# Stacking the left-over rows of two more groups in the Fourier stage of a spectral + gated block

## The chip, the cores and the metric

The kernel runs on one core of one Trainium2 chip. The metric is the device time of one execution in microseconds (us), given as the median of several executions. The core has five engines that run their own instruction lists and meet at semaphores: TensorE (PE in the profile, with its weight loads as PEld), VectorE (DVE), ScalarE (ACT), GpSimd (POOL) and SyncE (SP), which here only starts DMA transfers. The engines' work areas are SBUF (128 partitions of ordinary on-chip memory) and PSUM (where TensorE writes its sums).

## The reference

`x` is 2048 x 640 in float32. The block normalises each row, takes a two-dimensional real Fourier transform over rows and features, multiplies by a complex filter, transforms back and adds the result to `x`. A gated layer with a residual follows.

```python
def _A_ref(x, w_r, w_i):
    B, S, D = x.shape
    X = jnp.fft.rfft2(x, axes=(-2, -1))
    X = X * (w_r + 1j * w_i)
    return jnp.fft.irfft2(X, s=(S, D), axes=(-2, -1))

h = x + _A_ref(_layernorm(x), A_w_r, A_w_i)                     # D = 640, 321 frequencies
n = _layernorm(h)
h2 = h + ((n @ B_w_gate) * (n @ B_w_up)) @ B_w_down             # 640 -> 1728 -> 640
```

## The kernel before

All transforms are matrix products with constant tables. The program has four stages: a first transform along the rows for 16 tiles of 128 rows (`s1_mm`, L263), the feature stage that the change touches, the transform back along the features and rows, and the gated layer, which takes the larger part of the time. The order of every engine's instructions is the order in which the Python code calls the helpers; nothing reorders them afterwards. A semaphore wait stands in front of an instruction where its data or its buffer needs one, and an engine that waits holds up everything behind that instruction in its list. SP's list is such a list too: a transfer that must wait holds back the later ones.

**Left-over rows.** After the first transform the features are cut into four classes (even or odd, real or imaginary part) of about 160 rows. 128 rows of each fill a matrix operand (`s1`), and some 32 rows of each are left over. `s1_rest` (L292) puts the left-overs of all four classes together into the 128 partitions of `rest`. So that a faster format of matrix product keeps float32's accuracy there, ACT rounds them to a high part (`rest_high`, L299) and DVE forms the low part by a subtraction (`rest_low`, L302). Both lie in `s1r`: 128 partitions x (high or low) x 16 groups x 128 columns.

**The feature stage.** It runs over 16 groups of 128 columns. For group g:
- `d_mm(g)` (L428) is the transform along the features: four products from `s1` (the profile shows them as `im<-tab,s` and `re<-tab,s`), then the left-over rows. A group that has no entry in `ST` takes six products of 322 columns from `s1r` (high and low part against a table in two parts; `re<-frt,s1r`). A group with an entry in `ST` takes four products of 160 to 194 columns from a *stacked* operand (`re<-frt,st`), in which each class has the high part, the low part and the high part again under one another in 99 partitions.
- `d_out(g)` (L460) copies the result to SBUF on ACT (tile `t`).
- `s2_mm(g)` (L467) is the rest of the transform along the rows; for groups 1 to 13 it writes the PSUM tile `u`, of which there is one (`bufs=1`, L473).
- `filt(g)` (L478) multiplies by the filter on DVE, in three instructions that read `u` and the filter tile `wts` (L484 to L486); the closure it returns adds the two products, `y + us` (L493): on GpSimd for group 0, on DVE for the others.
- `is2_mm(g)` (L514) starts the way back; `is2_parts(g)` (L547) copies its sums out: `high` and `end` on ACT (L545), `low` on DVE (L563), `main` on ACT (L556), `edges` on GpSimd.

A round g of the loop at L583 calls `s2_mm(g)`, `d_mm(g+2)`, `is2_mm(g-1)`, then `filt(g)`, and behind it the copies and the sum. In round 0 ACT makes the high part for groups 10 to 15, in round 1 DVE makes their low part. The tile `qr`, into which `high` and `low` write, lies in the same memory as `rest`, so `high(0)` must wait until DVE has read `rest` for the last time.

**How the stacked operand is made.** A stacked operand needs rows in other partitions than they were computed in, and the kernel moves them through device memory: `spread(a, b)` (L443) writes the left-over rows of groups a to b-1 to the buffer `sfar` with four transfers of 66 pieces, `stack(g, n, ...)` (L448) reads n groups back with two transfers, of 264 and 132 pieces. A piece is as long as the number of groups in the call times 512 bytes. All are started by SP, between the loads of the matrices `mm` (`bits` in the profile) and of the filter (`load_w`, L407).

```python
PLAIN, MID = 5, 10
AGAIN = {0: (5, 3, "dC"), 1: (8, 2, "qt"), 4: (10, 3, 0), 7: (13, 3, 1)}
```

Groups 0 to 4 are not stacked. Groups 5 to 9 are written ahead of the loop, groups 10 to 15 in round 2. `AGAIN` says in which round which groups are read back, and to which memory.

Of the kernel before, what the change touches and what calls it, by code (L numbers as in the profile page):

```python
# [12 lines left out]
F32R = mybir.dt.float32r  # L13
AF = mybir.ActivationFunctionType
OP = mybir.AluOpType

P = 128
S, D, NF, FF = 2048, 640, 321, 1728
NT = S // P
NG = 16  # L20
# [6 lines left out]
RW = (160, 194, 162, 162)  # L27
PLAIN, MID = 5, 10
IPLAIN, IFAR = 5, 9
SUMS = 7  # L30
IPARTS = ((5, 4), (9, 3), (12, 4))
AGAIN = {0: (5, 3, "dC"), 1: (8, 2, "qt"), 4: (10, 3, 0), 7: (13, 3, 1)}
NR = 4
# [16 lines left out]
def f32(ap):  # L50
    return ap.bitcast(F32)
# [29 lines left out]
def tile_spectral_glu(ctx: ExitStack, tc: tile.TileContext, x, wre, wim, wgu, wlast, wdown, wdlast,  # L81
                      cc, ci, fmain, frem, imain, irem, mm, out):
    nc = tc.nc
# [52 lines left out]
    def home(tag, shape, name, dt=F32):  # L136
        return keep.tile(shape, dt, tag=tag, name=name)
# [11 lines left out]
    s1r = home("wA", [P, 2, NG, P], "s1r", F32R)  # L149
# [250 lines left out]
    s1_rest(NT - 1)  # L400
    for a, b in ((0, 2), (2, PLAIN), (PLAIN, MID)):
        rest_high(a, b)
        rest_low(a, b)
# [39 lines left out]
    def spread(a, b):  # L443
        for q, (r, s) in enumerate(RROWS):
            nc.sync.dma_start(sfar[q, :, :, a - PLAIN:b - PLAIN].rearrange("l r g n -> r l g n"),
                              f32(s1r[r:r + 32 * s + 1:s, :, a:b]))

    def stack(g, n, tag):  # L448
        if tag in (0, 1):
            o = s1r[:, tag, NG - 12:NG].rearrange("p (q n) m -> p q n m", q=4)  # L450
        else:
            o = home(tag, [P, 4, n, P], "st", F32R)
        src = sfar[:, :, :, g - PLAIN:g - PLAIN + n].rearrange("q l r g n -> q (l r) (g n)")
        for a, b, r in ((0, 66, 0), (66, 99, 0)):
            nc.sync.dma_start(f32(o[a:b].rearrange("p q g n -> p q (g n)")),
                              src[:, r:r + b - a].rearrange("q r n -> r q n"))
        for i in range(n):
            ST[g + i] = o[:, :, i]
# [19 lines left out]
    def filt(g):  # L478
# [11 lines left out]
        else:  # L490
            for h in range(2):
                products(h, PU[g][h][:, 0:NQ])
        return lambda: (tt if g else nc.gpsimd.tensor_tensor)(y, y, us, op=OP.add)  # L493

# [78 lines left out]
    for g in range(4):  # L573
        for way in range(2):
            load_mm(g, way)
        if g < 3:
            load_w(g)
    spread(PLAIN, MID)
    d_mm(0)
# [3 lines left out]
    for g in range(NG - 1):  # L583
# [32 lines left out]
        if g + 3 < NG:  # L616
            load_w(g + 3)
        if g >= 4 and g in AGAIN:
            stack(*AGAIN[g])
        if g == 0:  # L620
# [4 lines left out]
        if g + 2 < NG:  # L625
# [7 lines left out]
            if 1 <= g < NG - 3:  # L633
                low()
                main(slice(0, 4))
                edges(nc.gpsimd)
        if g < 2:
            stack(*AGAIN[g])
        elif g == 2:
            spread(MID, NG)  # L640
        if g == 9:
# [920 lines left out]
```

## Time and profile before

| | |
|---|---|
| median of 3 executions | 671.65 us (671.63 to 671.98) |
| the profiled execution, its own time | 671.61 us |
| its span, first to last instruction | 669.8 us |
| TensorE busy in the span | 660.0 us (99%) |
| TensorE in the chain that ended last | 95% of the span |
| granted TensorE clock | 1.00 throughout |
| feature stage | from about 38 us to 106 us |
| round with six left-over products (rounds 1 and 2) | 4.45 us each |
| round with four (rounds 3 and 4) | 3.99 and 3.98 us |

The time of the profiled execution is 1.8 us more than its span; that part lies outside the instructions that the profile shows. A row of the timeline view gives the start in the span, the duration, the engine, the source line, the operation, its tiles (output, arrow, inputs), shape and count; in brackets the engine's idle time before it and what ended it. A row of the windows view gives for one stretch of time the busy time of each engine with its number of instructions, then the granted clock, the mean share of the 16 DMA engines that was busy, and GB/s. "SPq" rows are transfers being started, not transferred.

### The profile page before, as it was taken

The numbers are of one execution on the slowest core, as the hardware profiler recorded it, in microseconds if no ns is written. First come the engines' busy times: TensorE is split into PE (matmuls) and PEld (weight loads), VectorE is DVE, ScalarE is ACT, GpSimd is POOL, SyncE is SP. The second block draws the span as 40 slices with busy tenths as digits, with TensorE's granted clock in tenths as the row PEclk, the third lists the DMA queues.
The fourth block names the chain that finished last, engine by engine and source line by source line (L and its number), as shares of the span: only waits on it lengthen the run. The fifth ranks groups of instructions, "written<-read, shape, count | busy, mean of one in ns | idle before, by whom it ended". The sixth has DMA issues, their size and how long they took to land.

```text
span 669.8 us, 10242 instructions
## 1 busy us (share of the span) xinstructions
PE 660.0 (99%) x3695; PEld 587.1 (88%) x3695; DVE 468.7 (70%) x951; ACT 321.6 (48%) x621; POOL 394.5 (59%) x379
## 2 busy tenths in 40 slices
PE   6999999999999999999999999999999999999997
PEld 6999999887888888888888899888888888888887
DVE  6969997788767767594857567754757475757644
ACT  6977773585525243453626146634434251624220
POOL 3101124750397977969686445198786869697610
PEclk9999999999999999999999999999999999999999
DMA  8639885502212120042332467212011121212004
GB/s 320 226 109 282 237 252 160 160 1 79 79 40 80 39 79 28 34 99 59 99 78 84 93 134 260 78 41 74 13 37 76 41 78 40 79 40 80 1 0 158
DMA packets 48953, 66.12 MB, mean 99 GB/s; under 512 B 24082, under 2 KB 30670, under 8 KB 48774
## 3 DMA queue, kind: packets, MB, share of 16 engines
q1 hardware_dynamic: 48246, 62.91, 30.5%
q0 software_dynamic: 288, 2.16, 0.8%
q8 instruction: 29, 0.48, 0.3%
q10 hardware_dynamic: 368, 0.39, 0.2%
q14 instruction: 22, 0.18, 0.1%
HBM read 54.61 MB, written 10.84 MB: 98 GB/s over the span
## 4 chain that ended last, share of the span: by engine, by line
PE 95%; ACT 2%; DVE 1%; DMA 1%; issue 0%; POOL 0%; DVEq 0%
PE e L121 50%; PE d L121 26%; PE eo L121 4%; PE y L121 2%; PE re L121 2%; PE u L476 2%; PE im L527 2%; PE im L121 2%; PE im L270 2%; PE ir L527 1%; DMA x<-in_x_dram 1%; ACT s L296 1%; ACT fold L212 0%; ACT fold L211 0%; PE y L803 0%; PE u L527 0%
## 5 line engine op out<-in xcount | busy, mean ns | idle before, releaser
L121 PE MATMUL e<-xt,wst 128*128 128x512 f32 x864 | 211.1, 390 | 0.0
L121 PEld LDWEIGHTS e<-xt,wst 128*128 128x128 f32 x864 | 160.6, 188 | 31.7
L1082 DVE TENSOR_TENSOR x<-d,x 128x320 f32<-128x320 f32 x280 | 120.5, 483 | 41.2 <-PE d L121 37.0
L121 PE MATMUL d<-wd,ht 128*128 128x320 f32 x832 | 142.2, 309 | 0.0
L121 PEld LDWEIGHTS d<-wd,ht 128*128 128x128 f32 x832 | 129.6, 188 | 5.2
L996 POOL TENSOR_TENSOR wst<-raw,wst 128x1024 fp32r<-128x1024 f32 x23 | 55.5, 2412 | 69.5 <-ACT wst L995 69.5
L121 PE MATMUL e<-t,wst 128*128 128x512 f32 x360 | 94.0, 391 | 0.0
L121 PEld LDWEIGHTS e<-t,wst 128*128 128x128 f32 x360 | 66.7, 188 | 13.0
L121 PE MATMUL d<-wt,ht 128*128 128x320 f32 x360 | 69.0, 309 | 0.0
L1012 POOL TENSOR_TENSOR wst<-raw,wst 128x896 fp32r<-128x896 f32 (+1 forms) x46 | 65.3, 1444 | 0.2 <-ACT wst L1007 0.2
L121 PEld LDWEIGHTS d<-wt,ht 128*128 128x128 f32 x360 | 57.3, 188 | 0.8
L1098 ACT ACTIVATE ht<-e 128x512 fp32r<-128x512 f32 x44 | 26.4, 599 | 49.2 <-DVE e L1160 23.7
L1007 ACT ACTIVATE wst<-raw 128x896 fp32r<-128x896 f32 (+1 forms) x48 | 30.1, 676 | 31.2 <-POOL raw L1001 30.5
L1156 DVE TENSOR_TENSOR e<-e,h 128x512 f32<-128x512 f32 x24 | 16.8, 699 | 39.3 <-ACT wst L1007 23.1
L1057 DVE TENSOR_TENSOR x<-d,x 128x320 f32<-128x320 f32 x62 | 27.5, 485 | 22.4 <-PE d L121 22.3
L688 ACT ACTIVATE wd<-draw 128x320 fp32r<-128x320 f32 (+1 forms) x30 | 15.7, 560 | 55.1 <-POOL draw L698 52.4
L121 PE MATMUL e<-xt,wdir 128*128 128x512 f32 x180 | 42.1, 392 | 0.0
L1136 ACT ACTIVATE h<-e 128x512 f32<-128x512 f32 x24 | 14.3, 596 | 56.8 <-PE e L121 56.8
L121 PEld LDWEIGHTS e<-xt,wdir 128*128 128x128 f32 x180 | 33.4, 188 | 7.7 <-ACT xt L813 0.5
L1101 DVE TENSOR_TENSOR ht<-e,ht 128x512 fp32r<-128x512 f32 x54 | 37.0, 686 | 1.6 <-ACT ht L1098 1.3
L1153 ACT ACTIVATE h<-e 128x512 f32<-128x512 f32 x24 | 14.3, 598 | 46.7 <-PE e L121 46.7
L667 POOL TENSOR_TENSOR wd<-draw,wd 128x640 fp32r<-128x640 f32 x8 | 12.4, 1576 | 40.8 <-ACT wd L666 40.8
(239 smaller groups left out, 1188.1 us busy)
## 6 DMA issues: line engine op xcount, KB each, us to landing
raw<-in_wgu_dram SPq DMA_DIRECT2D x24, 640.0 KB
draw<-in_wdown_dram SPq DMA_DIRECT2D x24, 320.0 KB
wts<-in_wre_dram SPq DMA_DIRECT2D x16, 322.0 KB
x<-in_x_dram SPq DMA_DIRECT2D x15, 320.5 KB
out_dram<-x SPq DMA_DIRECT2D x15, 320.0 KB
bits<-in_mm_dram SPq DMA_DIRECT2D x32, 128.0 KB
wts<-in_wim_dram SPq DMA_DIRECT2D x9, 322.0 KB
zfar<-zr SPq DMA_DIRECT2D x32, 80.0 KB
```

Of the source, the lines that this page charges most:

```text
L121: nc.tensor.matmul(o, l, r, start=start, stop=stop, skip_group_check=True)
L527: nc.tensor.matmul(out, y[:, h, a:b], inv(g, h), start=n == 0, stop=n == len(ys) - 1)
L688: act(o[:, 0, a:a + n], src, AF.Copy)
L996: ptt(wa[:, 1], stage[:, 0:1024], f32(wa[:, 0]), op=OP.subtract)
L1007: act(ws[:, 0, o:o + b - a], stage[:, a:b], AF.Copy)
L1012: ptt(ws[:, 1, o:o + b - a], stage[:, a:b], f32(ws[:, 0, o:o + b - a]), op=OP.subtract)
L1057: tt(xv, ps[b][:, 0:320], xv, op=OP.add)
L1082: tt(xv, o, xv, op=OP.add)
L1098: act(hop[:, a, 0], src, AF.Copy)
L1101: engine.tensor_tensor(hop[:, a, 1], src, f32(hop[:, a, 0]), op=OP.subtract)
L1136: act(h0, oa, AF.Copy)
L1156: tt(ob, ob, h1, op=OP.add)
```

## The change

Groups 3 and 4 become stacked groups as well.

- `PLAIN` is 3 instead of 5. The rows of groups 3 to 5 are written first, by four transfers, then read back at once in two calls (group 3 alone, then groups 4 and 5), and only then are the rows of groups 6 to 9 written. All of it stands on SP ahead of the loop. For this, high and low parts are made in the order (0, 1), (3, 4, 5), (2), (6 to 9).
- The other calls are cut anew: groups 6 and 7 are read in round 1, 8 in round 2, 9 to 11 in round 3, 12 to 14 in round 6, 15 in round 9. The rows of groups 10 to 15 are still written in round 2, from an earlier place in the code of that round, which is the same place in SP's list: behind the filter load of the round.
- A stacked operand can now be written in parts (`SH` keeps the tile, `at` gives the place). The transfers' shapes are those of before, but for the number of groups in them.
- The sum of group 1 is on GpSimd instead of DVE.

```diff
-PLAIN, MID = 5, 10
+PLAIN, NEXT, MID = 3, 6, 10
-AGAIN = {0: (5, 3, "dC"), 1: (8, 2, "qt"), 4: (10, 3, 0), 7: (13, 3, 1)}
+FIRST = ((3, 1, "dC", 0), (4, 2, "dC", 1))
+AGAIN = {1: ((6, 2, "qt", 0),), 2: ((8, 1, "dC", 0),), 3: ((9, 3, 0, 0),), 6: ((12, 3, 1, 0),), 9: ((15, 1, "dC", 0),)}
...
-    for a, b in ((0, 2), (2, PLAIN), (PLAIN, MID)):
+    for a, b in ((0, 2), (PLAIN, NEXT), (2, PLAIN), (NEXT, MID)):
         rest_high(a, b)
         rest_low(a, b)
...
-    def stack(g, n, tag):
-        if tag in (0, 1):
-            o = s1r[:, tag, NG - 12:NG].rearrange("p (q n) m -> p q n m", q=4)
-        else:
-            o = home(tag, [P, 4, n, P], "st", F32R)
-        src = sfar[:, :, :, g - PLAIN:g - PLAIN + n].rearrange("q l r g n -> q (l r) (g n)")
-        for a, b, r in ((0, 66, 0), (66, 99, 0)):
-            nc.sync.dma_start(f32(o[a:b].rearrange("p q g n -> p q (g n)")),
-                              src[:, r:r + b - a].rearrange("q r n -> r q n"))
+    SH = {}
+
+    def stack(g, n, tag, at):
+        if tag not in SH:
+            SH[tag] = s1r[:, tag, NG - 12:NG].rearrange("p (q n) m -> p q n m", q=4) if tag in (0, 1) else home(
+                tag, [P, 4, 3 if tag == "dC" else n, P], "st", F32R)
+        o = SH[tag][:, :, at:at + n]
+        src = sfar[:, :, :, g - PLAIN:g - PLAIN + n].rearrange("q l r g n -> (l r) q (g n)")
+        for a, b in ((0, 66), (66, 99)):
+            nc.sync.dma_start(f32(o[a:b].rearrange("p q g n -> p q (g n)")), src[0:b - a])
...
-        return lambda: (tt if g else nc.gpsimd.tensor_tensor)(y, y, us, op=OP.add)
+        return lambda: (tt if g > 1 else nc.gpsimd.tensor_tensor)(y, y, us, op=OP.add)
...
-    spread(PLAIN, MID)
+    spread(PLAIN, NEXT)
+    for job in FIRST:
+        stack(*job)
+    spread(NEXT, MID)
     d_mm(0)
...
-        if g >= 4 and g in AGAIN:
-            stack(*AGAIN[g])
+        if g == 2:
+            spread(MID, NG)
+        if g >= 4:
+            for job in AGAIN.get(g, ()):
+                stack(*job)
...
-        if g < 2:
-            stack(*AGAIN[g])
-        elif g == 2:
-            spread(MID, NG)
+        if g < 4:
+            for job in AGAIN.get(g, ()):
+                stack(*job)
```

The order of instructions on SP, from the end of the first loads into round 1, before (`sfar<-s1r` writes the left-over rows, `st<-sfar` reads them back; `bits` are the matrices, `wts` the filter):

```order
L445 DMA sfar<-s1r 33x2x640 x4
L417 DMA bits<-in_mm_dram 128x256
L410 DMA wts<-in_wre_dram 128x644
L455 DMA st<-sfar 66x4x384
L455 DMA st<-sfar 33x4x384
L417 DMA bits<-in_mm_dram 128x256 x2
L410 DMA wts<-in_wre_dram 128x644
```

and with the change:

```order
L446 DMA sfar<-s1r 33x2x384 x4
L458 DMA st<-sfar 66x4x128
L458 DMA st<-sfar 33x4x128
L458 DMA st<-sfar 66x4x256
L458 DMA st<-sfar 33x4x256
L446 DMA sfar<-s1r 33x2x512 x4
L418 DMA bits<-in_mm_dram 128x256
L411 DMA wts<-in_wre_dram 128x644
L418 DMA bits<-in_mm_dram 128x256 x2
L411 DMA wts<-in_wre_dram 128x644
```

Four reads and four writes now stand ahead of the matrix of group 4 and the filter of group 3 (the first `bits` and `wts` rows), where one set of four writes stood.

DVE in rounds 1 and 2, before, from the first filter product of group 1 to that of group 2:

```order
L484 TENSOR_TENSOR y<-u,wts 128x644
L485 SCALAR_TENSOR_TENSOR us<-u,wts 64x644
L486 TENSOR_TENSOR us<-u,wts 64x644
L303 TENSOR_TENSOR s1r<-rest,s1r 128x768
L493 TENSOR_TENSOR y<-y,us 128x644
L563 TENSOR_TENSOR qr<-ir_647,qr 64x32x8
L484 TENSOR_TENSOR y<-u,wts 128x644
```

and with the change:

```order
L486 TENSOR_TENSOR y<-u,wts 128x644
L487 SCALAR_TENSOR_TENSOR us<-u,wts 64x644
L488 TENSOR_TENSOR us<-u,wts 64x644
L304 TENSOR_TENSOR s1r<-rest,s1r 128x768
L565 TENSOR_TENSOR qr<-ir_653,qr 64x32x8
L486 TENSOR_TENSOR y<-u,wts 128x644
```

The sum `y<-y,us` of group 1 is gone from here; GpSimd's list has it behind the sum of group 0.

TensorE in round 1, `d_mm(3)` and what follows it, with the change (before, the four rows with `st` were six rows with `s1r`, 128x322 each):

```order
L478 MATMUL u<-t,bits 128x322 x2
L122 MATMUL im<-tab,s_89 128x160
L122 MATMUL re<-tab,s_89 128x193
L122 MATMUL im<-tab,s_89 128x161
L122 MATMUL re<-tab,s_89 128x161
L122 MATMUL im<-frt,st 128x160
L122 MATMUL re<-frt,st 128x194
L122 MATMUL im<-frt,st 128x162
L122 MATMUL re<-frt,st 128x162
L529 MATMUL ir_653<-bits,y 65x32x4 x2
```

Here `u` is `s2_mm(1)`, `ir` the beginning of `is2_mm(0)`.

## The prediction

> **What bounds the kernel now.** I read first the windows of rounds 1 to 4, then what TensorE waits for, then each engine's timeline in rounds 1 to 3.
>
> ```profile
> 45.58:50.03 4.45, 4.45 (x33) 4.12 (x31) 3.75 (x6) 2.60 (x6) 1.55 (x1) 1.00 0.66 174
> 50.03:54.48 4.45, 4.45 (x32) 4.12 (x31) 4.29 (x7) 3.36 (x8) 0.74 (x2) 1.00 0.95 288
> 54.48:58.47 3.99, 3.99 (x31) 3.66 (x29) 3.56 (x6) 2.79 (x7) 0.74 (x2) 1.00 0.93 246
> ...
> PE eo L121 <- POOL qr L560: 0.3, 1, 0.3
> ```
>
> TensorE is busy for the whole of each round, and the last row is the only wait of TensorE between 30 and 200 us: the stage runs at TensorE's speed, at a clock of 1.00. But round 2 has DVE busy for 4.29 of 4.45 us, so it is nearly a second bound, and the DMA engines are at 0.95.
>
> ```profile
> 47.70 0.42 PE L121 MATMUL re<-frt,s1r 128*128 128x322 f32 x1
> ...
> 52.16 0.42 PE L121 MATMUL re<-frt,s1r 128*128 128x322 f32 x1
> ...
> 53.16 0.60 PE L527 MATMUL ir<-bits,y 128*65 128x128 f32 x4
> 53.59 1.06 PE L527 MATMUL im<-bits,y 128*128 128x128 f32 x8
> ...
> 54.48 1.25 PE L476 MATMUL u<-t,bits 128*128 128x322 f32 x4
> ...
> 56.61 0.35 PE L121 MATMUL im<-frt,st 99*128 99x160 f32 x1
> ...
> 57.13 0.60 PE L527 MATMUL ir<-bits,y 128*65 128x128 f32 x4
> ```
>
> Matmuls overlap, so a block's cost is the distance from its first start to the next block's. Group 4's six left-over products take 53.16 - 52.16 = 1.00 us; group 5's four stacked ones 57.13 - 56.61 = 0.52 us.
>
> **The change part by part.**
>
> *Fewer products on TensorE.* 1.00 - 0.52 = 0.48 us for each of groups 3 and 4, on the path: 0.96 us at most. (The rounds say nearly the same: 4.45 - 3.99 = 0.46.) Whether all of it is kept depends on the tile `u`, of which there is one.
>
> ```profile
> 48.57 0.82 DVE L486 TENSOR_TENSOR us<-u,wts 64x644 f32<-64x644 f32 x1
> 49.42 0.96 DVE L303 TENSOR_TENSOR s1r<-rest,s1r 128x768 fp32r<-128x768 f32 x1
> 50.29 0.82 DVE L493 TENSOR_TENSOR y<-y,us 128x644 f32<-128x644 f32 x1
> 51.16 0.42 DVE L563 TENSOR_TENSOR qr<-ir,qr 64x256 fp32r<-64x256 f32 x1
> 51.61 0.83 DVE L484 TENSOR_TENSOR y<-u,wts 128x644 f32<-128x644 f32 x1
> ...
> 53.32 0.82 DVE L486 TENSOR_TENSOR us<-u,wts 64x644 f32<-64x644 f32 x1
> ...
> 55.77 0.83 DVE L484 TENSOR_TENSOR y<-u,wts 128x644 f32<-128x644 f32 x1 [0.32 <-PE u L476]
> ...
> 50.47 0.38 ACT L545 ACTIVATE qr<-ir 64x256 fp32r<-64x256 f32 x1 [0.84 <-DVE s1r L303]
> ...
> 52.06 0.60 ACT L556 ACTIVATE qm<-im 128x512 f32<-128x512 f32 x1
> ```
>
> DVE runs without a gap here and lets go of `u` at 53.32 + 0.82 = 54.14. TensorE writes `u` for group 3 at 54.48, only 0.34 later. With both savings it would come at 54.48 - 0.96 = 53.52 and find `u` still in use.
>
> *The sum moved to GpSimd* takes 50.29 to 51.11 out of DVE's list, but DVE does not gain 0.82 us. Its next instruction, L563 of group 0, needs `high(0)` on ACT, and that waits (the bracket) for DVE's L303, which ends at 49.42 + 0.96 = 50.38 as before: `high(0)` stays at 50.47 to 50.85. Handing over cost 0.09 us there (50.38 to 50.47), so L563 starts at about 50.93 instead of 51.16: 0.23 us earlier. `filt(2)` behind it keeps its length, so `u` comes free at 54.14 - 0.23 = 53.91, and TensorE, with a hand-over of 0.05 to 0.1, writes it at about 54.0. Before that was 54.48, so **0.48 us of the 0.96 are kept**, and TensorE stands for some 0.45 us ahead of `s2_mm(3)`. That is the new wait I expect.
>
> Is the rest of it lost later, or won back? `filt(3)` then waits for TensorE's `u` as it does at 55.77, and the whole pattern runs 0.48 us earlier: `u` is free again 2.53 us behind that start (51.61 to 54.14 in round 2), and TensorE is back 3.99 us after its last `u`. Nothing is late twice, nothing is regained. One smaller wait disappears inside the first: `is2_mm(1)` would write its `im` bank at 53.59 - 0.96 = 52.63, and ACT's `main(0)` reads the bank of group 0 until 52.66.
>
> *GpSimd's new sum* is priced by the old one, and by a pair of rows from a later stage:
>
> ```profile
> 46.33 1.55 POOL L493 TENSOR_TENSOR y<-y,us 128x644 f32<-128x644 f32 x1 [18.11 <-DVE us L486]
> ...
> 110.30 0.50 DVE L755 TENSOR_TENSOR yt<-q 128x322 f32<-128x322 f32 x1
> ...
> 110.35 1.06 POOL L763 TENSOR_TENSOR yt<-q 128x318 f32<-128x318 f32 x1 [1.62 <-DVE q L759]
> ...
> 128.77 0.75 POOL L763 TENSOR_TENSOR yt<-q 128x318 f32<-128x318 f32 x1
> ```
>
> It starts when DVE's L486 ends (48.57 + 0.82 = 49.39) and takes 1.55 us: 50.95. Beside it runs DVE's L303. Where GpSimd's L763 starts 0.05 us behind a DVE sum of two SBUF operands, it takes 1.06 us, else 0.75, so I let it lose the overlap with L303 too, up to 0.92 us: 51.9. `is2_mm(1)` needs the sum at 53.16 - 0.96 = 52.20. It stays hidden, and the waits around `u` would cover another 0.45 us; if that cover were gone, each further 0.1 us would cost 0.1.
>
> *Group 3's rows in time?* This is the unknown that matters: they are due at 47.70, in round 1.
>
> ```profile
> 40.39 0.83 DVE L303 TENSOR_TENSOR s1r<-rest,s1r 128x640 fp32r<-128x640 f32 x1
> ...
> 41.25 2.54 SPq L445 DMA_DIRECT2D sfar<-s1r  x4
> ...
> 45.26 0.35 SPq L410 DMA_DIRECT2D wts<-in_wre_dram  x1
> 46.63 0.75 SPq L455 DMA_DIRECT2D st<-sfar  x2
> ...
> 106.52 1.91 SPq L716 DMA_DIRECT2D ifar<-qr  x4
> 108.48 0.57 SPq L719 DMA_DIRECT2D ifar<-qr  x1
> 110.54 0.30 SPq L727 DMA_DIRECT2D xt<-ifar  x1
> ...
> 121.06 0.32 SPq L727 DMA_DIRECT2D si<-ifar  x1
> ...
> 121.00:122.00 1.00, 1.00 (x9) 1.00 (x9) 0.96 (x3) 0.27 (x1) 1.00 (x2) 1.00 0.08 32
> ...
> 125.00:126.00 1.00, 1.00 (x6) 0.76 (x5) 0.87 (x2) 1.00 (x3) 0.79 (x2) 1.00 0.34 92
> 126.00:127.00 1.00, 1.00 (x8) 0.92 (x8) 0.71 (x1) 1.00 (x3) 1.00 (x2) 1.00 0.00 0
> ```
>
> The second subtraction on DVE has the same 384 columns as before and is done when the third starts (40.39). The first write can be issued at about 40.4. From first write to the read that waited for it: 46.63 - 41.25 = 5.4 us with five groups and another load between; 110.54 - 106.52 = 4.0 us for the later stage's copy with 2 KB pieces. From the last of those writes to the read: 2.1 us. So the read of group 3 is issued between 40.4 + 1.2 (three issues ahead of the last at about 0.4 us) + 2.1 = 43.7 and 45.8; three groups have 3/5 of the bytes, and I take 44.2.
>
> The read: the `si` pair has the same 396 pieces in the same two shapes, three groups long, on an empty queue. Issued at 121.06, its data flow from about 122 (DMA share 0.08 in the slice before) to some 125.5 (0.34, then 0.00): 0.9 us of start, 3.5 us of transfer. Group 3 alone has a third of the bytes. If bytes count, 0.9 + 1.2 + up to 0.5 for the landing = 2.6 us; if pieces count, 0.9 + 3.5 + 0.3 = 4.7. The landing lies between 43.7 + 2.1 = 45.8 and 45.8 + 4.7 = 50.5. I take bytes: **44.2 + 2.6 = 46.8, in time by 0.9 us**. A lateness up to 0.45 us would cost nothing, since it only takes the place of the wait for `u`.
>
> *The rest of SP's list.* Reads of groups 4 and 5 (issued at about 45, due at 47.70 + 4.45 - 0.48 = 51.67) have 6.7 us, where `si` with half as many bytes again takes some 4.7. The writes of groups 6 to 9 and the two extra reads stand ahead of group 3's filter load, issued at 45.26 before. Two more reads, about 0.4 us of issue each, and four writes at 2.54 move it from 45.26 to some 49 or 50. The stack reads and writes ahead of it put its landing at 53 to 54, against `filt(3)` at 55.3. It is covered by one to two microseconds; without that cover a late filter costs its lateness. The extra left-over traffic (two groups more) meets DMA engines that have 5 to 7% free in rounds 2 and 3, and later filter loads have about two rounds of lead. One more ACT and one more DVE instruction at 39.6 to 41.3 us lie ahead of a DVE pause and cost nothing.
>
> Sum: -0.48. The profiled execution becomes 671.61 - 0.48 = 671.13 us (span 669.3); its own time is 0.04 below the median, so the median becomes 671.65 - 0.48 = **671.2 us**. That is -0.07%, inside the 0.2% (1.34 us) that a measurement of this kernel can tell from no change.
>
> **The rivals.**
>
> *All 0.96 us are kept* (670.7): if `u` came free by 53.52. For it: DVE loses 0.82 us of work. Against it: the bracket on ACT's row, which pins `high(0)` and L563 behind it.
>
> *Pieces, not bytes, set the read; group 3 is late.* Then it lands at 44.2 + 4.7 = 48.9, 1.2 us late; 0.45 of that replaces the wait for `u`, so 0.48 - 0.75 = 0.27 us are lost: 671.9, slower than before. It decides from a landing of 47.70 + 0.45 + 0.48 = 48.6. With the upper end 50.5 the loss is 2.8 - 0.45 - 0.48 = 1.9: 673.5. For it: the piece count stays at 396 while pieces shrink to 512 bytes, and every transfer seen here has a start of about a microsecond. Against it: `si` has 178 GB/s at a DMA share of 0.68, the sort of figure that bytes explain.
>
> ```profile
> 122.00:125.00 3.00, 3.00 (x22) 2.68 (x20) 2.96 (x8) 2.01 (x5) 2.94 (x3) 1.00 0.68 178
> ```
>
> On this the Trainium skill's page "DMA: Bandwidth & Descriptors", section "Anatomy of one DMA — SWDGE (gpsimd) path", has a fit of 2.0 us plus bytes at 436 GB/s for one transfer. As an estimate by it, `si`'s first part (396 KB) takes 2.9 us and group 3's (132 KB) 2.3; the trace's pair took over 4, so the fit, made for another path, is too fast here, and the sum does not use it.
>
> *The filter of group 3 or the matrices behind it are late*: landing at 56.5 instead of 53.5 would hold `filt(3)`, and so `u`, by 1.2 us: about 672.3.
>
> *GpSimd's sum starts first and holds DVE up.* A later stage shows a small DVE instruction held beside a sum on GpSimd, 0.77 us instead of 0.17:
>
> ```profile
> 32.35 0.17 DVE L214 TENSOR_SCALAR ve<-sq 128x2 f32<-128x2 f32 x1
> ...
> 139.29 0.75 POOL L763 TENSOR_TENSOR yt<-q 128x318 f32<-128x318 f32 x1
> ...
> 139.30 0.77 DVE L214 TENSOR_SCALAR ve<-sq 128x3 f32<-128x3 f32 x1
> ...
> 45.77 0.49 DVE L486 TENSOR_TENSOR us<-ir,wts 64x322 f32<-64x322 f32 x1
> ```
>
> Then L303 would wait up to 1.55 us, and `high(0)`, L563 and `u` with it: 54.0 + 1.6 against 54.48, a loss of 1.1: 672.7. Against it: DVE issues L303 0.03 us behind L486, while GpSimd took 0.07 to follow DVE in round 0 (45.77 + 0.49 = 46.26 to 46.33). The Trainium skill's page "SBUF — State Buffer", section "SBUF: two separate sides", states the mechanism: whichever of a GpSimd instruction and a DVE instruction with two SBUF inputs starts first holds a shared port for its whole length, and the other "fully blocks". The trace shows a little less than that: by the rule the L763 at 110.35 would have ended at 110.80 + 0.75 = 111.55, and it ended at 111.41.
>
> **How the numbers follow.** The forecast (0.3 to 0.6 us faster, 671.0 to 671.4) 0.50; all kept, or nearly (670.6 to 671.0) 0.14; group 3 late 0.20, of which a quarter beyond 673.0; the filter late 0.09, a fifth beyond; GpSimd first 0.04; a gain that no row shows 0.03. The range goes from 670.6 to 672.4 and leaves out about 0.15. Faster by over 0.2% needs more than the 0.96 us there are: 0.04. Slower by over 0.2% is the tail of the late transfers: 0.08. Within 0.2%: 0.88.
>
> **What would show it.** In the changed profile: `d_mm(3)` and `d_mm(4)` with four `st` products each, 0.52 us a block; the first write at about 40.4 and group 3's read at about 44.2; no wait ahead of `d_mm(3)`'s `st` products at 47.7; a wait of about 0.4 us for DVE's L486 ahead of `s2_mm(3)`, which starts at about 54.0; L563 of group 0 at about 50.9; and everything from 56 us on earlier by a constant 0.5 us. A wait of TensorE on a DMA in round 1, or DVE waiting for the filter at 55, would make the prediction wrong on the slow side; `s2_mm(3)` at 53.5 on the fast side.

## The result, and the profile after

The changed kernel takes 675.97 us (median of 6 executions, 674.65 to 677.17) against 671.58 us (671.24 to 671.98) for the kernel before: a ratio of 1.0064, 95% interval 1.0054 to 1.0074. It is 4.4 us slower, where about 0.5 us faster was forecast, and 3.6 us above the top of the range. Single executions of 1082, 1713 and 2359 us, far outside all others, are left out of the comparisons below. The profiled execution took 677.17 us with a span of 675.4 us; it is the slowest of the six, so its loss of 5.6 us of span is read for the place of the loss rather than for its usual size.

The windows of the changed kernel, cut at each start of TensorE's `u` (rounds 1 to 9). Columns: stretch, its length, busy time of PE, PEld, DVE, ACT and POOL with the number of instructions, granted clock, DMA share, GB/s.

```profile
45.71:49.78 4.07, 4.07 (x30) 3.65 (x29) 3.37 (x6) 2.60 (x6) 1.72 (x2) 1.00 0.52 136
49.78:54.42 4.64, 4.22 (x29) 3.74 (x29) 3.74 (x6) 3.68 (x10) 2.83 (x3) 1.00 1.04 326
54.42:58.47 4.05, 4.05 (x28) 3.72 (x29) 3.69 (x6) 2.37 (x6) 0.73 (x2) 1.00 0.98 255
58.47:63.63 5.16, 4.28 (x30) 3.74 (x29) 4.48 (x6) 2.98 (x8) 0.73 (x2) 1.00 0.72 220
63.63:67.61 3.98, 3.98 (x30) 3.65 (x29) 3.03 (x5) 2.97 (x8) 0.73 (x2) 1.00 0.91 300
67.61:71.73 4.12, 4.12 (x30) 3.67 (x29) 3.66 (x6) 3.11 (x8) 0.73 (x2) 1.00 0.94 216
71.73:78.30 6.57, 4.31 (x30) 3.76 (x29) 3.73 (x6) 4.80 (x12) 0.73 (x2) 0.99 0.97 310
78.30:83.94 5.64, 5.64 (x28) 4.84 (x29) 4.22 (x6) 1.03 (x3) 0.73 (x2) 0.71 1.00 234
83.94:87.92 3.98, 3.98 (x30) 3.65 (x29) 3.30 (x6) 2.98 (x8) 0.73 (x2) 1.00 0.64 203
```

Rounds 1 and 2 are shorter than before together (8.71 against 8.90 us). Three rounds are long: round 4 by 1.18 us, round 7 by 2.58 and round 8 by 1.66 against the 3.98 to 3.99 us of such a round before. With 0.13 for round 6 and -0.13 for rounds 1 to 3 that makes 5.42 of the 5.6 us; another 0.13 is that round 1 began later (45.71 against 45.58). Behind round 9 the two executions run in step.

What TensorE waited for (engine, line, releaser: us in total, times, longest), and the rows of its timeline that matter:

```profile
PE u L478 <- issue: 2.3, 1, 2.3
...
PE im L122 <- DMA st<-sfar: 0.9, 1, 0.9
...
PE u L478 <- DVE us L488: 0.4, 1, 0.4
```

```profile
47.84 0.35 PE L122 MATMUL im<-frt,st 99*128 99x160 f32 x1
...
48.36 0.60 PE L529 MATMUL ir<-bits,y 128*65 128x128 f32 x4
...
61.82 0.31 PE L122 MATMUL im<-frt,st 99*128 99x160 f32 x1 [0.88 <-DMA st<-sfar]
...
78.30 2.48 PE L478 MATMUL u<-t,bits 128*128 128x322 f32 x4 [2.26 <-issue]
```

The stacked rows of group 6 came late (61.82). The wait of 2.26 us at 78.30 is put down to "issue", but DVE's and GpSimd's timelines show what it was:

```profile
49.56 0.96 DVE L304 TENSOR_TENSOR s1r<-rest,s1r 128x768 fp32r<-128x768 f32 x1
51.30 0.42 DVE L565 TENSOR_TENSOR qr<-ir,qr 64x256 fp32r<-64x256 f32 x1 [0.79 <-ACT bits L547]
...
75.67 0.83 DVE L486 TENSOR_TENSOR y<-u,wts 128x644 f32<-128x644 f32 x1 [2.72 <-DMA wts<-in_wre_dram]
...
77.37 0.82 DVE L488 TENSOR_TENSOR us<-u,wts 64x644 f32<-64x644 f32 x1
...
49.60 2.32 POOL L495 TENSOR_TENSOR y<-y,us 128x644 f32<-128x644 f32 x1 [1.59 <-DVE us L488]
```

DVE waited 2.72 us for the filter of group 7. So it let go of `u` at 77.37 + 0.82 = 78.19, and TensorE could write `u` for group 8 only then. The filter was late for the most part because SP had started its load late. SP's timeline with the change, and, behind it, what SP itself waited for between 40 and 76 us (SP's line, releaser: us in total, times, longest), first with the change, then before:

```profile
40.49 2.54 SPq L446 DMA_DIRECT2D sfar<-s1r  x4
44.89 1.60 SPq L458 DMA_DIRECT2D st<-sfar  x4
46.53 2.44 SPq L446 DMA_DIRECT2D sfar<-s1r  x4
...
49.63 0.39 SPq L411 DMA_DIRECT2D wts<-in_wre_dram  x1
...
52.86 0.95 SPq L458 DMA_DIRECT2D st<-sfar  x2
...
56.13 5.49 SPq L446 DMA_DIRECT2D sfar<-s1r  x4
...
67.68 0.38 SPq L411 DMA_DIRECT2D wts<-in_wre_dram  x1
```

```profile
SPq L458 <- DMA sfar<-s1r: 3.1, 3, 1.7
SPq L413 <- DMA s1r<-sfar: 2.1, 1, 2.1
SPq L446 <- DMA wts<-in_wim_dram: 1.7, 1, 1.7
...
SPq L446 <- DMA st<-sfar: 1.0, 1, 1.0
```

```profile
SPq L417 <- PE im L527: 10.6, 7, 2.5
...
SPq L455 <- DMA sfar<-s1r: 0.9, 1, 0.9
...
SPq L417 <- DMA s1r<-sfar: 0.2, 1, 0.2
```

Before, SP mostly stood because a buffer was still in use by TensorE, which means that it was ahead; it waited 1.1 us on transfers. With the change it waits 11.8 us on transfers (all rows of that view with DMA). The load of group 7's filter goes out at 67.68 instead of 63.08 us; it is then also under way for longer, 7.53 instead of 4.80 us.

**Why SP stands.** The program gives its transfers eight semaphores in turn, so a transfer waits until the eighth before it has landed. The list of SP's instructions, with what each waits for, at the four writes that took 5.49 us:

```
L446 DMA sfar<-s1r 33x2x768 [waits DMAHW7_49,Activation_49]
L446 DMA sfar<-s1r 33x2x768 [waits DMAHW0_49]
L446 DMA sfar<-s1r 33x2x768 [waits DMAHW1_49]
L446 DMA sfar<-s1r 33x2x768 [waits DMAHW2_49]
L458 DMA st<-sfar 66x4x128 [waits DMAHW3_49]
```

The trace records every increment of these semaphores, which gives the moment at which each transfer landed. With the change (us):

```
third write issued      59.01   eighth before it: filter, imaginary part   landed 58.99
fourth write issued     60.81   eighth before it: first read, groups 6, 7  landed 60.79
read of group 8 issued  61.70   eighth before it: second read, groups 6, 7 landed 61.68
```

SP goes on within 0.02 us of each landing. The two reads of groups 6 and 7, issued at 52.86 and 53.23, were under way for 7.9 and 8.5 us.

### The profile page after: what moved, and what is told of

Same layout as the page of the kernel before. It is cut to its first block, busy times and chain, and to the rows that moved or that the text cites. A ratio compares the mean times of both kernels' runs of the same rounds, so it can differ in the third digit from the quotient of the medians.

```text
span 675.4 us, 10255 instructions
## 1 busy us (share of the span) xinstructions
PE 662.9 (98%) x3691; PEld 588.7 (87%) x3691; DVE 468.1 (69%) x951; ACT 321.5 (48%) x622; POOL 396.2 (59%) x380
## 4 chain that ended last, share of the span: by engine, by line
PE 91%; DMA 3%; ACT 2%; DVE 2%; SPq 1%; issue 1%; POOL 0%; DVEq 0%
PE e L122 50%; PE d L122 26%; PE eo L122 4%; PE y L122 2%; PE u L478 2%; PE im L529 2%; PE im L271 2%; DMA st<-sfar 1%; PE re L122 1%; PE im L122 1%; DMA sfar<-s1r 1%; PE ir L529 1%; DMA x<-in_x_dram 1%; ACT s L297 1%; ACT fold L213 0%
```

## The experiments

Each was timed beside the kernel before, whose median was 671.5 to 671.7 us each time. Two theories stood at first: the order in SP's list (Q), or too little room for the traffic (V). The first four kernels only ask which part of the change matters.

**The products alone.** Kernel before, with four products for groups 3 and 4 and no transfers for them.

```diff
+    for g in (3, 4):
+        ST[g] = s1r[:, 0, 0:4]
     for g in range(NG - 1):
```

> The kernel before, with the four stacked products for groups 3 and 4 taken from rows that lie in SBUF already (no row of these groups is written to or read from device memory; the left-over part of these two groups is therefore not computed rightly). Transfers and their order are those of before, the sum of group 1 stays on DVE. Theory T (the extra transfers ahead of the filter loads make the change slow): 671.58 less 0.2 to 0.5 us, 671.1 to 671.4, and no wait of TensorE on a transfer. Rival P (stacking more groups costs TensorE time itself, through u and DVE): slower than 671.6, towards 676.

Measured 671.35 us, ratio 1.0002 (0.9994 to 1.0011); the profiled execution, 671.35, lies 0.26 below that of the kernel before. One wait of 0.4 us at `u` appears. The shorter blocks cost nothing; a gain of about 0.2 us in the medians (671.35 against 671.53) is not told from none, since the interval holds 1.

**The transfers alone.** The changed kernel, in which groups 3 and 4 are written and read back but use their six products.

```diff
-            ST[g + i] = o[:, :, i]
+            if g + i > 4:
+                ST[g + i] = o[:, :, i]
```

> The changed kernel with all its transfers in their order, but groups 3 and 4 take the six products of before (their rows are written and read back and not used). Theory T: the loss is there without the gain: about 676.0 + 0.2 = 676 us, 675 to 677, with TensorE waiting for the rows of group 6 and for u behind a late filter load. Rival P: about 671.6.

Measured 676.54 us, ratio 1.0074 (1.0057 to 1.0092). The whole loss is there without a single product changed. In this profile the rows of group 6 are in time, against what was expected; the filter of group 7 landed at 74.14, 1.9 us after DVE had come to it (72.26), and the granted clock falls behind it (last section). The profiles of the sum on DVE, one group and the later writes, below, have the late filter and no wait for group 6 either. So the late rows of round 4 may belong to the slowest execution of the changed kernel and not to its usual loss.

**The layout of the buffer in device memory.** Kernel before, with the two groups more in `sfar` that nobody uses.

```diff
-    sfar = far.tile([4, 2, 33, NG - PLAIN, P], F32, name="sfar")
+    sfar = far.tile([4, 2, 33, NG - PLAIN + 2, P], F32, name="sfar")
```

> The kernel before with the buffer in device memory made for 13 groups instead of 11, so that its rows lie 6656 bytes apart as in the change and not 5632; nothing else differs. Rival L (the new layout slows the reads, and with them the queue): 673 to 676 us. Theory T: 671.6, within 0.4.

Measured 671.58 us, ratio 1.0002 (0.9993 to 1.0010): not the layout.

**The sum of group 1 back on DVE.**

```diff
-        return lambda: (tt if g > 1 else nc.gpsimd.tensor_tensor)(y, y, us, op=OP.add)
+        return lambda: (tt if g else nc.gpsimd.tensor_tensor)(y, y, us, op=OP.add)
```

> The changed kernel with the sum of group 1 back on DVE. Rival G (the sum on GpSimd, which took 2.32 us instead of 1.55, causes the loss): 671 to 672 us. Theory T: 675.5 to 676.9, as with the change.

Measured 674.39 us, ratio 1.0047 (1.0031 to 1.0063), still with a late filter. The sum is not the cause; whether it adds the 1.6 us between the medians can't be told, since the intervals overlap.

**The read of groups 9 to 11 a round later**, so that it stands behind the filter load of group 7 in SP's list.

```diff
-AGAIN = {1: ((6, 2, "qt", 0),), 2: ((8, 1, "dC", 0),), 3: ((9, 3, 0, 0),), 6: ((12, 3, 1, 0),), 9: ((15, 1, "dC", 0),)}
+AGAIN = {1: ((6, 2, "qt", 0),), 2: ((8, 1, "dC", 0),), 4: ((9, 3, 0, 0),), 6: ((12, 3, 1, 0),), 9: ((15, 1, "dC", 0),)}
```

> The changed kernel with the reads of groups 9 to 11 in round 4, behind that round's filter load, instead of round 3. Theory Q (what stands ahead of a filter load in SP's list decides): the filter of group 7 no longer waits behind them, and its wait (2.7 us of DVE, then the slow clock) goes: 672 to 674 us, with a wait for the rows of group 6 left that comes and goes. Rival V (the added bytes alone decide, wherever they stand): unchanged, 675 to 677.

Measured 674.84 us, ratio 1.0054 (1.0036 to 1.0072). The wait moved to the read itself:

```profile
75.54 0.47 PE L122 MATMUL im<-frt,s1r 99*128 99x160 f32 x1 [2.85 <-DMA s1r<-sfar]
```

Theory Q falls in this form: what is moved back becomes what is late.

**The left-over transfers of the rounds on GpSimd's queue**, out of SP's list.

```diff
-            spread(MID, NG)
+            spread(MID, NG, nc.gpsimd)
...
-                stack(*job)
+                stack(*job, nc.gpsimd)
```

> The changed kernel with the left-over transfers inside the loop (reads of groups 6 and up, writes of groups 10 to 15) started by GpSimd on its own queue instead of SP. Same bytes; SP's list holds matrices and filter loads alone from round 0 on. Theory Q: 671 to 673 us, with the filter loads issued as early as before. Rival V: 674 to 677.

Measured 678.59 us, ratio 1.0097 (1.0082 to 1.0111). No filter load is late any more, but the rows are, by more. A queue of its own makes no room.

```profile
76.90 0.47 PE L122 MATMUL im<-frt,s1r 99*128 99x160 f32 x1 [3.95 <-DMA s1r<-sfar]
```

**One group instead of two**, group 4 alone.

```diff
-PLAIN, NEXT, MID = 3, 6, 10
-FIRST = ((3, 1, "dC", 0), (4, 2, "dC", 1))
+PLAIN, NEXT, MID = 4, 6, 10
+FIRST = ((4, 2, "dC", 0),)
```

> The changed kernel with only group 4 stacked in addition: group 3 is neither written nor read and takes its six products. One group less in the first write (0.13 MB) and its read (0.2 MB, two transfers) gone. Theory Q and V: the first block ends about 1.6 us earlier on SP, so the loss shrinks: 672 to 674.5 us. If only the cut of the later reads mattered (groups 6 to 15, the same here): 675 to 677.

Measured 673.80 us, ratio 1.0041 (1.0030 to 1.0053): half the loss for half the change, with a wait of DVE on the filter of 1.6 us.

**Other cuts of the calls**: groups 3 and 4 in one read, 5 to 7, 8 and 9, 10 to 12 and 13 to 15 in the others. This is four left-over transfers fewer.

```diff
-PLAIN, NEXT, MID = 3, 6, 10
+PLAIN, NEXT, MID = 3, 5, 10
...
-FIRST = ((3, 1, "dC", 0), (4, 2, "dC", 1))
-AGAIN = {1: ((6, 2, "qt", 0),), 2: ((8, 1, "dC", 0),), 3: ((9, 3, 0, 0),), 6: ((12, 3, 1, 0),), 9: ((15, 1, "dC", 0),)}
+FIRST = ((3, 2, "qt", 0),)
+AGAIN = {0: ((5, 3, "dC", 0),), 2: ((8, 2, "qt", 0),), 4: ((10, 3, 0, 0),), 7: ((13, 3, 1, 0),)}
```

> Groups 3 and 4 written and read in one go ahead of everything, and all later groups cut and read as in the kernel before, but for groups 8 and 9, which are read in round 2 instead of round 1. Fewer and longer transfers in rounds 0 to 3 than in the changed kernel, the same bytes. Theory Q: the filter load of group 7 stands ahead of the read of groups 10 to 12 again: 671.2 to 673. Rival V: 674 to 677.

Measured 673.13 us, ratio 1.0028 (1.0018 to 1.0038). The same rows in fewer and longer transfers give 2.8 of the 4.4 us back, so it is not the rows alone.

**As many bytes less as the change added.** The changed kernel without the second read from group 6 on; the products of these groups use 66 rows and leave out what that read carries.

```diff
-            mmx(ps[b][:, o:o + w], ST[g][0:99, q], frall[0:99, a:a + w], False, q >= 2)
+            k = 66 if g >= 6 else 99
+            mmx(ps[b][:, o:o + w], ST[g][0:k, q], frall[0:k, a:a + w], False, q >= 2)
...
-        for a, b in ((0, 66), (66, 99)):
+        for a, b in ((0, 66), (66, 99))[:1 if g >= 6 else 2]:
```

> The changed kernel, but the second read of every stacked call from group 6 on (33 rows, the repeated high part) is left out and the left-over products of those groups use 66 rows instead of 99; the part of these groups' left-over products that the second read carries is missing from the result. About 0.68 MB less is read, which is what the change added (0.66 MB). The order in SP's list, the first block of reads and writes ahead of the loop, and the instruction counts of TensorE stay. Theory V (the DMA engines have no room for the added bytes between 41 and 75 us): the filter loads come in time again, 671.2 to 672.2 us. Theory Q (the longer block in front of group 3's filter load, or the order of the list, is what hurts): 674 us or more. In between (672.5 to 673.5) would mean that bytes are half of it.

Measured 671.94 us, ratio 1.0004 (0.9995 to 1.0013). No transfer is waited for by TensorE; only the forecast wait at `u` is left:

```profile
PE u L479 <- DVE us L489: 0.4, 1, 0.4
```

**A fourth place for the filter**, so that group 3's is loaded in the idle stretch before 40 us and the loads up to that of group 10 go out a round earlier.

```diff
+    early = cut(tab, 676, 2, NQ)
...
+    def load_re(g):
+        nc.sync.dma_start(early if g in (3, 7) else wts[:, (g % 4 if g < 8 else g + 1) % 3], wre[g])
...
-        nc.sync.dma_start(w, wre[g])
...
+        if g == 2:
+            load_re(3)
...
+        if g < 7:
+            load_re(g + 4)
```

> The changed kernel with a fourth place for the filter's real part, in a corner of a table's memory that is free until round 9. Group 3's filter is then loaded with the first three, at 25 to 41 us, when the DMA engines stand nearly idle, and the later loads come one round earlier. The bytes and the left-over transfers stay those of the changed kernel; some 0.33 MB leave the crowded stretch. Theory V (no room): half of the added bytes are bought back and each filter load has a round more of lead, so 671.2 to 672.5 us, no wait of DVE on a filter load above 0.3 us; the rows of groups 6 or 9 may still be some 0.5 us late. Theory Q (SP's list alone): the loads move ahead in SP's list, too, so about the same; what tells them apart is the read of group 6, which by V comes earlier (under 0.4 us of wait of TensorE) and by Q stays at about 0.9 us.

Measured 672.53 us, ratio 1.0018 (1.0009 to 1.0027): 3.4 us back with all bytes and all left-over transfers in place. How much of it is the load in the idle stretch and how much the round more of lead for the loads behind it, this kernel does not separate. DVE never waits for a filter. TensorE does not wait for group 6 any more; it waits 0.39 us for rows of groups 9 to 11:

```profile
73.15 0.31 PE L122 MATMUL im<-frt,s1r 99*128 99x160 f32 x1 [0.39 <-DMA s1r<-sfar]
```

**Both the other cuts and the fourth place** (the two edits above together).

> The h_front cut of the calls (groups 3 and 4 read together, 5 to 7, 8 and 9, 10 to 12, 13 to 15) with the fourth place for the filter. It is the version that should keep what the products save. Theory V: with 0.33 MB moved into the idle stretch the remaining waits of h_front (0.5 to 0.6 us on filter loads, 0.6 on rows) go, 671.0 to 671.8 us. If it stays at 673 as h_front did, lead and room are not the cause of those waits.

Measured 673.01 us, ratio 1.0023 (1.0013 to 1.0033): a miss, no better than the other cuts alone. In the profiled execution (676.51 us, the slowest of eleven) the rows of group 5 are 2.96 us late, the filter of a later group 1.17; a place more for filters does not help rows.

At this point V, in the form "too many bytes", explained most. Three kernels put it to the test, since the changed kernel also leaves the DMA engines less busy between 45 and 50 us (0.46 against 0.67).

**The bytes without the change.** Kernel before with two loads of 330 KB more that nobody reads.

```diff
             load_w(g + 3)
+        if g in (1, 3):
+            nc.sync.dma_start(cut(tab, 676, 2, NQ), wre[g])
```

> The kernel before with two loads more, of 330 KB each, behind the filter loads of rounds 1 and 3: a part of the filter is read a second time into a corner of memory that nobody reads until round 9. No left-over transfer, no product and no sum is changed. Theory V1 (the added bytes are enough): 0.66 MB more in the crowded stretch gives filter loads or rows that come late, 673 to 676 us. Theory V2 (the change hurts because its first block leaves the DMA engines half idle at 40 to 50 us, and the bytes alone would still fit): 671.4 to 672.2 us.

Measured 671.71 us, ratio 1.0006 (0.9997 to 1.0015). The bytes alone cost nothing that can be told.

**The second writes behind the filter load of group 3.**

```diff
-    spread(NEXT, MID)
     d_mm(0)
...
             load_w(g + 3)
+        if g == 0:
+            spread(NEXT, MID)
```

> The changed kernel with the four writes of groups 6 to 9 behind group 3's matrix and filter loads instead of ahead of them. All bytes stay. The filter load of group 3 is then issued at about 47 instead of 49.6 us and the stretch up to 50 us is filled better. Theory V1 (bytes): still 673.5 to 676 us, the lateness moves to the rows of group 6 or a later load. Theory V2 (the unused room): 671.3 to 672.8 us.

Measured 676.12 us, ratio 1.0066 (1.0054 to 1.0078), though the filter load of group 3 went out at 46.54. V2 falls; so did V1 with the bytes above.

**That and the fourth place together.**

> The changed kernel with the fourth place for the filter (as in i_slot) and the later writes (as in l_late). If the two remedies are for two causes they add up: 671.2 to 671.9 us, no wait on a transfer between 45 and 90 us. If they are for one, it stays near i_slot's 672.5 us.

Measured 672.80 us, ratio 1.0020 (1.0011 to 1.0030): as the fourth place alone.

**The number of transfers without the bytes.** Kernel before with eight loads of 8 KB more, the number that the change adds up to round 3.

```diff
+    def tiny(j):
+        nc.sync.dma_start(cut(tab, 676, 4, P)[16 * (j // 4):16 * (j // 4) + 16, j % 4], wre[0][0:16, 0, 0:P])
+    for j in range(6):
+        tiny(j)
     d_mm(0)
...
             spread(MID, NG)
+            tiny(6)
+            tiny(7)
```

> The kernel before with eight tiny transfers more (16 rows of 512 bytes each, into a corner of memory that nobody reads until round 9): six behind the writes ahead of the loop, two behind the writes of round 2. That is the number of transfers that the change adds up to round 3, with none of its bytes. Theory N (SP has at most eight transfers under way, and more of them means that SP stands): SP waits several us more on earlier transfers, some filter load late, 673 to 675 us. Theory L (a left-over transfer is long for its bytes, and that is what fills the queue): 671.4 to 672.0 us.

Measured 671.93 us, ratio 1.0007 (0.9999 to 1.0016). The number alone costs nothing that can be told either.

**The number of the changed kernel with the bytes of the shortened one.**

```diff
-        for a, b in ((0, 66), (66, 99)):
+        for a, b in ((0, 66), (66, 67 if g >= 6 else 99)):
```

> As k_bytes, but the second read of the calls from group 6 on is still there, with one row instead of 33: the number of transfers is that of the changed kernel, the bytes those of k_bytes (products of 66 rows there, so this part of the result is missing). Theory N (slots): back to 674 us or more, as the changed kernel. Theory L (the time that the 33-row reads take): as k_bytes, 671.6 to 672.6 us.

Measured 673.41 us, ratio 1.0025 (1.0014 to 1.0037): 2.6 us below the changed kernel, 1.5 above the kernel without these transfers. Neither theory as written; both a read's duration and its mere presence count.

What ties these together is the lead of a filter load: the time from its landing to the moment at which DVE could use it. Before, DVE uses group 7's and group 8's filter without waiting at

```profile
71.72 0.83 DVE L484 TENSOR_TENSOR y<-u,wts 128x644 f32<-128x644 f32 x1
...
75.71 0.83 DVE L484 TENSOR_TENSOR y<-u,wts 128x644 f32<-128x644 f32 x1
```

The landings are from the semaphore increments, in one profiled execution of each kernel; "usable" is the start of that instruction, less its wait where it waited for the load (us; "both" is the kernel with both dummies, below):

```
                                     issued  landed  usable   lead
group 7  before                       63.08   67.88   71.72    3.8
         two loads of 330 KB more     63.83   69.62   71.73    2.1
         eight tiny loads more        65.30   69.75   71.91    2.2
         both                         65.98   71.54   72.01    0.5
         changed, no second reads     64.48   70.99   71.56    0.6
         changed, tiny second reads   66.64   73.08   72.41   -0.7
         changed                      67.68   75.21   72.95   -2.3
group 8  before                       67.08   72.94   75.71    2.8
         two loads of 330 KB more     67.09   74.82   75.72    0.9
         eight tiny loads more        67.80   75.39   75.90    0.5
         both                         69.03   76.74   75.85   -0.9
```

Each dummy eats 1.7 to 2.3 us of the lead and does not show in the time, because the lead was 2.8 to 3.8. The change eats 3.8 + 2.3 = 6.1 us at group 7. Two last kernels ask whether the delays add up, with nothing of the change in them.

**Both dummies in the kernel before** (the tiny loads in another corner, so that the two don't meet).

> The kernel before with both dummies: the two extra loads of 330 KB (rounds 1 and 3) and the eight tiny transfers. Theory S (a lead of some 3.2 us that delays eat one after another): the two delays, 1.5 us and 2.4 us, add to about 3.9, the load of group 7's filter lands some 0.7 us late, 672.0 to 673.5 us, with a wait of DVE on that load of 0.3 to 1.5 us. Theory A (the dummies are harmless because they are not left-over rows that somebody waits for; the change's loss comes from its reads and writes as such): no wait on a filter load, 671.6 to 672.1 us.

Measured 673.31 us, ratio 1.0030 (1.0015 to 1.0046); the executions lie between 671.60 and 677.25, the profiled one at 673.01. At group 7 the delays add to 3.4 us, as 1.7 and 1.7 singly; at group 8 to 3.7, against 1.9 + 2.3. The load that came late was group 8's, not group 7's as expected:

```profile
76.83 0.83 DVE L484 TENSOR_TENSOR y<-u,wts 128x644 f32<-128x644 f32 x1 [0.98 <-DMA wts<-in_wre_dram]
```

**Four loads of 330 KB instead of two**, and the eight tiny ones.

```diff
+        if g in range(4):
+            nc.sync.dma_start(cut(tab, 676, 2, NQ), wre[g])
```

> As m_both, with four extra loads of 330 KB (rounds 0 to 3) instead of two. Theory S: another 1.5 us or more of delay, so 2 to 3.5 us late in all, 673.5 to 676 us, with a wait of DVE on a filter load of 1.5 to 3 us and a TensorE stand behind it, as in the changed kernel. Theory A: 671.6 to 672.3 us.

Measured 676.99 us, ratio 1.0081 (1.0067 to 1.0094), a little more than expected. Part of it is the kernel's own doing: one dummy waited 3.1 us for the one before it, which has the same place in memory, and SP stood with it. The signs are those of the changed kernel, a filter 3.38 us late and the same stand:

```profile
72.19 0.83 DVE L484 TENSOR_TENSOR y<-u,wts 128x644 f32<-128x644 f32 x1 [3.38 <-DMA wts<-in_wre_dram]
...
74.82 2.49 PE L476 MATMUL u<-t,bits 128*128 128x322 f32 x4 [3.01 <-issue]
```

So a loss of this kind needs no additional left-over row, only enough delay on the DMA queue: the theory that delays eat a lead until it is gone holds. No version beat the kernel before; the products without their transfers, the most that could be had, lie 0.2 us below it and are not told from it.

**What stays open.** Which share of the delay comes from the left-over transfers' use of only some DMA engines (last section) was not tried. Nor is it known why one execution of the changed kernel is 2.5 us longer than another; before, where every load has lead, the spread is 0.7.

## Why the prediction was wrong, point by point

- **Products.** Right. 48.36 - 47.84 = 0.52 us for group 3's four, and the same for group 4's.
- **What of it is kept.** The mechanism was right (the forecast wait of 0.4 us at `u` is there), its size was off. DVE's L565 did not come 0.23 us earlier: its row at 51.30 waits for ACT's L547 that writes `bits`, which is the second of ACT's two copies (`end`), and not only for the first. By `s2_mm(3)` 54.48 - 54.42, plus 0.13 by which this execution started later, makes 0.19 us kept instead of 0.48. It is the 0.34 us that TensorE came behind the release of `u` before, less the 0.15 between release (53.45 + 0.82 = 54.27) and write now.
- **GpSimd's sum.** Right: 2.32 us, between the bounds of 1.55 and 2.47 and near the upper one; it ended at 51.92 (51.9 forecast) and is needed at 52.50. The rule quoted from the Trainium skill's page "SBUF — State Buffer", section "SBUF: two separate sides", gives DVE's end at 50.52 plus 1.55 = 52.07; here the trace agrees within 0.15 us, on the short side. DVE started first, so the rival in which GpSimd does fell.
- **Group 3's rows.** Right: written from 40.49, read from 44.89 (44.2 forecast), landed at 47.59 by the semaphore, needed at 47.84. In time by 0.25 us rather than 0.9. The flight of 2.7 us is that of "bytes" (2.6); the rival of "pieces" (4.7) fell.
- **Filter of group 3.** Issued at 49.63 as forecast (the sum counts two reads ahead of it where the change has four; 45.26 + 4 x 0.4 + 2.54 gives 49.4), landed at 55.15 (53 to 54 forecast), used from 55.84: in time by 0.7 us instead of one to two. The rival of this late load did not happen here; it happened four groups later.
- **The step that failed** stands under "The rest of SP's list": "The extra left-over traffic (two groups more) meets DMA engines that have 5 to 7% free in rounds 2 and 3, and later filter loads have about two rounds of lead", priced at nothing. Two rounds are the time from the issue of a load to its use (63.08 to 71.72, 8.6 us). From landing to use it was 3.8 us for group 7 and 2.8 for group 8, because these loads were under way for 4.8 and 5.9 us. Against that the change set 4.6 us of later issue (63.08 to 67.68) and 2.7 us of longer flight (4.80 to 7.53): 7.3 us, of which 1.2 did no harm because DVE itself came to the filter that much later (72.95). The wait that this term had at nothing was 2.72 us of DVE and 2.26 of TensorE. The rows of group 6 were missed in the same way: their read was given no term, and it was under way for 8.5 us.
- **What followed.** The late rows made round 4 longer by 1.18 us, the late filter round 7 by 2.58, and the granted clock round 8 by 1.66; the prediction has no term for a clock below 1.00.

The sentence that should have given warning was its own: where the engines have 5% free, two groups more come as delay, and then the lead that is to cover it has a size that must be measured.

## What to carry to other kernels

Where the DMA engines are nearly full, price an added transfer by the lead of every later transfer in the same queue, counted from landing to use and not from issue, and add up what eats it: time on the engines, and places among the transfers that may be under way at once. That something costs nothing while a lead lasts tells nothing about the next thing; two dummies, each harmless, together cost 1.6 us. Of all versions that kept the added rows, the one that moved a load into an idle stretch and gave the next ones a round more of lead gave most back, 3.4 us; new orders within the full stretch gave 1.1 at most, and fewer, longer transfers 2.8.

## What the runs showed of the hardware

**Left-over transfers complete on 11 of the 16 DMA engines.** A load of 128 rows ends with 16 increments of its semaphore; a left-over write or read (66 or 33 rows) has one increment 0.5 to 1.4 us behind its issue and then 11. In the changed kernel, for the filter load issued at 55.66 (between left-over reads and writes) and for the write issued at 56.13:

```
load   59.00 59.10 59.13 59.16 59.25 | 60.57 60.70 60.92 61.05 61.23 61.58 61.71 61.95 62.13 62.38 62.94
write  56.65 | 60.99 61.42 61.64 61.75 61.85 62.33 62.44 62.58 62.84 63.09 63.69
```

Five engines deliver the load at 59.0 to 59.25, eleven only 1.3 to 3.7 us later, behind left-over rows, as it seems, that the five don't carry. The Trainium skill's page "DMA: Bandwidth & Descriptors", section "Why a DMA increments its semaphore by 16 and not by 1", states the rule: a transfer runs on the largest number of engines up to 16 that divides the slowest dimension of both its sides, here its rows, so 11 for 66 and 33, and the sequencer posts the missing increments at once. The trace agrees with both, and with the DMA share of 0.68 (11/16 = 0.69) that the prediction quoted from 122 to 125 us. So a mean share of 0.95 may hide engines with no room at all; no view here gives the share of a single engine. That rows in a multiple of 16 would be faster here is an inference; no run shows it.

**The granted clock falls behind a stand of TensorE, on a fixed grid.**

```profile
74.71:78.12 3.41, 1.32 (x12) 1.13 (x10) 2.41 (x3) 2.98 (x7) 0.00 (x0) 1.00 0.92 325
78.12:81.53 3.41, 3.23 (x8) 2.47 (x9) 2.04 (x4) 0.00 (x0) 0.73 (x2) 0.50 1.00 212
```

These are windows of the changed kernel. Behind the stand of 2.26 us the clock is 0.50 for 3.41 us; the products of `u` take 2.48 us instead of 1.25, and 1.66 us are lost on top of the wait. The same followed stands of 1.98 us (the transfers alone), 2.35 (the later writes), 2.85 (the read a round later), 3.01 (four loads more) and 3.95 (GpSimd's queue), but not one of 1.23 (one group), and not one of 2.96 us, from 56.69 to 59.64, in the kernel with both the other cuts and the fourth place:

```profile
55.02:58.43 3.41, 1.67 (x10) 1.26 (x9) 3.13 (x5) 1.01 (x2) 0.74 (x2) 1.00 1.07 280
58.43:61.84 3.41, 2.20 (x18) 2.15 (x19) 0.59 (x1) 1.42 (x4) 0.00 (x0) 1.00 0.82 272
```

The length of the stand alone does not decide. In each of the six traces with such a fall in this stage, the clock changes a whole number of 3.413 us after the first entry of its record (here at 6.44; 78.12 is 21 of them later and 81.53 is 22). The windows above are cut on this grid. In the slice ahead of each of the six falls TensorE was busy for 0.17 to 1.44 us, and for 0 to 1.38 us ahead of the fall that ends each of the twenty traces, behind the last products; from 1.67 us on, in any slice at full clock behind 15 us of all twenty traces, there was no fall. The stand of 2.96 us lay across two slices and left 1.67 us of work in the first and 2.20 in the second.

The page "TensorE: Matmul & The Clock Gate" of the Trainium skill, section "Part 1: The HAM clock gate (the "warmup" mystery)", has half the clock after an idle window of about 3.4 us that runs freely. The traces agree with the half, the length and the free run; they differ in that the window need not be idle, since 1.44 us of work in it did not prevent the fall.
